# Dummy matmuls up to and between the first transposes, and two small matmuls moved into the last output matmuls of block 0

## The chip, the cores and the metric

The kernel runs on one core of a Trainium2 chip. The metric is the device time of one execution in microseconds (us), as the median of several runs. The engines are TensorE (PE; its weight loads are listed apart as PEld), VectorE (DVE), ScalarE (ACT), GpSimd (POOL) and SyncE (SP), which here only issues DMAs.

## What is computed

A linear attention is followed by a gated feed-forward layer, for 8 batches of 576 tokens with 8 heads of 64 (so 512 columns) and 1536 hidden units. Inputs and output are float32; the matmuls run in float16.

```python
q_s = exp(q) / sum(exp(q), axis=-1)            # over the 64 of a head
k_s = exp(k) / sum(exp(k), axis=2)             # over the 576 tokens
kv  = einsum('bhsd,bhse->bhde', k_s, v)
x   = einsum('bhsd,bhde->bhse', q_s, kv)       # rows: 8*576 tokens of 512
out = (gelu(x @ w_gate) * (x @ w_val)) @ w_out
```

## The kernel before, in words

Every batch has 512 main tokens and 64 remaining ones. A "block" is the feed-forward of one batch's main tokens; block 8 holds the remaining tokens of all batches. The order is 0 to 6, 8, 7.

**Attention of a batch b.** `exp` (L139) runs on ACT and writes eq (from q) and ek (from k). `norm` (L170) divides eq by its row sums, a head pair hp at a time: `norm_sum` (reduce and reciprocal, always DVE) and `norm_mul` (L165, DVE or POOL). `cast_v` (L148) makes v float16 on DVE, ACT or POOL; on POOL, spans of more than two heads are cut into calls of two. `unit_kv(b, g)` (L189) has 10 matmuls, 5 for each of two head pairs, into the PSUM tile pskv, then on DVE one reciprocal rck and two kv_sb. `unit_t(b, g)` (L213) transposes the eq of two head pairs with 8 transposes on PE into pst, and copies pst to eqt. `unit_x(b, hp)` (L242) is one matmul of kv_sb with eqt into psx, then a cast to xt on the engine named. g=0 are the lower heads (hp 0 and 1), g=1 the upper ones.

**Feed-forward of a block.** For each of 12 slices fi of the hidden units there are 4 matmuls into psg and 4 into psv (L266 to L269), then `gate` (L271): Gelu on ACT, and a product on DVE that gives ht. `ffn_first` (L286) begins blocks 0 and 1: it runs the halves of several slices that need only xt of hp 0 and 1, and calls the rest of the batch's attention in between. Then come the output matmuls (L310): for each of 4 row groups ns, 12 matmuls into psy, and `evac` (L345), which scales psy into yo; two row groups are stored together. Block 0 does all four row groups in two passes: fi 0 to 5 for each, then fi 6 to 11 for each (L491 to L500).

**Order of the work.** It is written out by hand: each engine runs its instructions in the order in which the program issues them. Pieces of other batches' work are put behind named points: `at(b, FI, i, ...)` behind slice i of block b, `at(b, NS, i, ...)` behind row group i, and `ride` (L476) calls them. In block 0, `NS` points 4 to 7 come behind the four row groups of the second pass. All loads go through SP in one order, with 5 buffers for q, k and v and 8 for staged weights. The weight casts are on POOL.

**The start (L386 to L415).** `warm_pe(n)` (L257) issues n matmuls of 512 columns with the identity as weights and zeros as data; nothing reads their result. Before, 16 of them come first, then the 8 transposes of the lower heads of batch 0, 6 more dummies, the 8 transposes of the upper heads, 20 matmuls of `unit_kv`, 4 of `unit_x`, and block 0.

PSUM has 6 banks for the tiles named "mm" (psg, psv, psy, pswarm, and psx where `big` is set) and 2 for the attention's.

Of the kernel before, what the change touches and what calls it, by code (L numbers as in the profile page):

```python
# [11 lines left out]
ACTF = mybir.ActivationFunctionType  # L12
ALU = mybir.AluOpType

_H_SCALE = 1024.0
# [3 lines left out]
def kernel(  # L19
# [10 lines left out]
    nc = tc.nc  # L30
# [6 lines left out]
    NFI = F // P  # L37
# [79 lines left out]
    def copy_on(eng, dst, src):  # L117
        if eng == "pool":
            nc.gpsimd.tensor_copy(out=dst, in_=src)  # L119
        elif eng == "act":  # L120
            nc.scalar.copy(out=dst, in_=src)  # L121
        else:
            nc.vector.tensor_copy(out=dst, in_=src)  # L123
# [15 lines left out]
    def exp(nm, b, h0=0, h1=H, n0=0, parts=((1, NC), (0, 1))):  # L139

        dst = (ek_b if nm == "k" else eq_b)[b % 2]
        for c0, c1 in parts if nm == "k" else ((n0, NC),):
            nc.scalar.activation(  # L143
                out=dst[:, c0:c1, h0 * D:h1 * D].rearrange("p n (h d) -> p h n d", d=D),
                in_=tiles[(nm, b)][:, h0:h1, c0 * D:c1 * D].rearrange("p h (n d) -> p h n d", d=D),
                func=ACTF.Exp, bias=kbias[:, 0:1] if c1 == 1 else 0.0)

    def cast_v(b, h0, h1, eng="pool"):  # L148
        if eng == "pool" and h1 - h0 > 2:
            for h in range(h0, h1, 2):  # L150
                cast_v(b, h, h + 2)
            return
        copy_on(eng, v16_b[b % 2][:, :, h0:h1, 0:D].rearrange("p n h d -> p h n d"),
                tiles[("v", b)][:, h0:h1, :].rearrange("p h (n d) -> p h n d", d=D))
# [15 lines left out]
    def norm(b, hp, eng="dve", n0=0):  # L170
        norm_sum(b, hp, n0)
        norm_mul(b, hp, eng)
# [16 lines left out]
    def unit_kv(b, g):  # L189
        pskv = ps_att.tile([P, 2, 2 * VW], f32, name="pskv", tag="att")  # L190
        for j in range(2):
            hp = 2 * g + j
            for n in range(NC):
                nc.tensor.matmul(  # L194
                    pskv[:, j, :], ek_b[b % 2][:, n, hp * P:(hp + 1) * P],
                    v16_b[b % 2][:, n, 2 * hp:2 * hp + 2, 0:VW],
                    start=(n == 0), stop=(n == NC - 1))
        rck = att.tile([P, 2], f32, name="rck", tag="rck")
        nc.vector.reciprocal(out=rck, in_=pskv[:, :, D])
        for j in range(2):  # L200
            kv_sb = att.tile([P, 2, D], f16, name="kv_sb", tag="kv", bufs=12)
            nc.vector.scalar_tensor_tensor(  # L202
                out=kv_sb,
                in0=pskv[:, j, :].rearrange("p (h e) -> p h e", e=VW)[:, :, 0:D],
                scalar=rck[:, j:j + 1], in1=mask, op0=ALU.mult, op1=ALU.mult)
            st[(b, "kv", 2 * g + j)] = kv_sb
# [6 lines left out]
    def unit_t(b, g, eng="dve"):  # L213
        eqt = get_eqt(b)
        pst = ps_att.tile([P, 2, MAIN], f16, name="pst", tag="att")
        for j in range(2):
            hp = 2 * g + j
            for n in range(NM):
                nc.tensor.transpose(  # L219
                    pst[:, j, n * P:(n + 1) * P],  # L220
                    eq_b[b % 2][:, n + 1, hp * P:(hp + 1) * P], ident)
        copy_on(eng, eqt[:, 2 * g:2 * g + 2, 0:MAIN], pst)
# [14 lines left out]
    def get_xt(b):  # L237
        if (b, "xt") not in st:
            st[(b, "xt")] = att.tile([P, HP, MAIN], f16, name="xt", tag="xt")
        return st[(b, "xt")]  # L240
# [16 lines left out]
    def warm_pe(n):  # L257
        ps = ps_big.tile([P, 512], f32, name="pswarm", tag="mm")
        for _ in range(n):
            nc.tensor.matmul(ps, ident, warm, start=True, stop=True)  # L260
# [18 lines left out]
    def ffn_fi(xt, fi):  # L279
        psg = ps_big.tile([P, 512], f32, name="psg", tag="mm")  # L280
        mm_gv(psg, wg_sb, xt, fi, range(HP))
        psv = ps_big.tile([P, 512], f32, name="psv", tag="mm")
        mm_gv(psv, wv_sb, xt, fi, range(HP))
        return gate(psg, psv)
# [25 lines left out]
    def mm_out(psy, hts, ns, fis):  # L310
        for fi in fis:
            nc.tensor.matmul(psy, hts[fi][:, ns * P:(ns + 1) * P], wo_sb[:, fi, :],  # L312
                             start=(fi == 0), stop=(fi == NFI - 1))
# [4 lines left out]
    def store(eng, src, b, n0, n1, c0=0, c1=C):  # L318
        base = out_rows(b)[:, 1 + n0:1 + n1, c0:c1]
        (pm, nm), (pn, _), _ = base.ap  # L320
        last = [[1, (n1 - n0) * C]] if c1 - c0 == C else [[1, c1 - c0]]
        eng.dma_start(out=bass.AP(tensor=base.tensor, offset=base.offset,
                                  ap=[[pm, nm], [NM * pn, 2]] + last), in_=src)
# [18 lines left out]
                    nc.scalar.activation(out=yl, in_=ps[i], func=ACTF.Copy, scale=1.0 / _H_SCALE)  # L342
                store(nc.scalar if i == 2 else nc.sync, yl, b, ns, ns + 1, c0, c1)

    def evac(b, ns, psy):  # L345
        if ns % 2 == 0:
            yo_t[b] = yop.tile([P, 2, C], f32, name="yo", tag="yo")
        yo = yo_t[b][:, ns % 2, :]
        if b == B:
            nc.vector.tensor_scalar(out=yo, in0=psy, scalar1=1.0 / _H_SCALE,  # L350
                                    scalar2=None, op0=ALU.mult)
            for j in range(2):
                nc.sync.dma_start(
                    out=out[(2 * ns + j) * S:(2 * ns + j + 1) * S, :].rearrange(
                        "(m n) c -> m n c", n=NT)[:, 0, :],
                    in_=yo[j * 64:(j + 1) * 64, :])
            return
        nc.vector.tensor_scalar(out=yo, in0=psy, scalar1=1.0 / _H_SCALE,  # L358
                                scalar2=None, op0=ALU.mult)
        if b == order[-1]:  # L360
            store(nc.sync, yo, b, ns, ns + 1)
        elif ns % 2 == 1:
            store(nc.sync, yo_t[b].rearrange("p n c -> p (n c)"), b, ns - 1, ns + 1)
# [24 lines left out]
    exp("q", 0, 4, 8, 1)  # L388
    exp("k", 0, 0, 4)
    exp("k", 0, 4, 8)  # L390
    warm_pe(16)
    norm(0, 0, "dve", 1)
    norm(0, 1, "pool", 1)
    norm(0, 2, "dve", 1)
    norm(0, 3, "pool", 1)
    unit_t(0, 0, "dve")
    warm_pe(6)
    cast_v(0, 0, 4, "dve")
    cast_v(0, 4, 6, "act")
    unit_t(0, 1, "act")  # L400
    cast_v(0, 6, 8, "dve")
    unit_kv(0, 0)
    unit_kv(0, 1)
    cast_w("wg", 0, "pool")
# [13 lines left out]
    FI, NS = 0, 1  # L418
    plan = {}

    def at(b, kind, i, *fns):
        plan.setdefault((b, kind, i), []).extend(fns)

    L = lambda f, *a: (lambda: f(*a))
# [3 lines left out]
       L(norm, 1, 0), L(norm, 1, 1, "pool"), L(norm_sum, 1, 2), L(norm_mul, 1, 2, "pool"),  # L428
       L(cast_v, 1, 0, 4, "act"), L(exp, "k", 1, 4, 8))
    at(0, NS, 5, L(unit_t, 1, 0))  # L430
    at(0, NS, 6, L(unit_kv, 1, 0), L(cast_v, 1, 4, 6, "act"), L(cast_v, 1, 6, 8),
       L(norm, 1, 3, "pool"))
    at(0, NS, 7, L(unit_x, 1, 0, "act", True), L(unit_x, 1, 1, "act", True),
       L(preload, ACTF.Gelu))
    first1 = [[L(unit_kv, 1, 1), L(unit_t, 1, 1)], [L(unit_x, 1, 2, "act")],
              [L(unit_x, 1, 3, "dve")]]
    first = {0: [[], []], 1: first1}
# [38 lines left out]
    def ride(b, kind, i):  # L476
        for fn in plan.get((b, kind, i), []):
            fn()

    for b in order:  # L480
        xt = get_xt(b) if b < B else xtr
        hts = []
        fi0 = 0
        if b in first:
            hts = ffn_first(xt, first[b])
            fi0 = len(hts)
            ride(b, FI, fi0 - 1)
        for fi in range(fi0, NFI):
            hts.append(ffn_fi(xt, fi))
            ride(b, FI, fi)  # L490
        if b == 0:  # L491
            psys = []
            for ns in range(4):
                psys.append(ps_big.tile([P, C], f32, name="psy", tag="mm"))
                mm_out(psys[ns], hts, ns, range(0, NFI // 2))
                ride(b, NS, ns)
            for ns in range(4):
                mm_out(psys[ns], hts, ns, range(NFI // 2, NFI))
                evac(b, ns, psys[ns])
                ride(b, NS, 4 + ns)  # L500
        else:
            for ns in range(4):
                if b == order[-1] and ns == 3:
                    last_rows(b, hts, ns)
                    break
                psy = ps_big.tile([P, C], f32, name="psy", tag="mm")
                mm_out(psy, hts, ns, range(NFI))
                evac(b, ns, psy)
                ride(b, NS, ns)
# [30 lines left out]
```

The softmax here doesn't subtract the row's maximum and nothing guards it: scores larger than these inputs give would overflow.

## Times and profile before

| what | value |
|---|---|
| median of 5 runs | 329.17 us (328.57 to 330.06) |
| the profiled execution | 329.04 us, span 327.2 us |
| PE busy | 317.6 us (97%) |
| DVE, ACT, POOL busy | 180.1, 147.3, 45.2 us |
| mean DMA rate over the span | 154 GB/s |

The span runs from the first to the last instruction. A matmul's record ends later than the next one begins, since they are pipelined, so spacing is read from the chain or from starts. In the timeline, a row gives the start, the length, the engine, the line, the operation, what is written and read, the number of merged instructions, and in brackets the idle time of the engine before it with what ended it. The granted TensorE clock is a share of full speed.

### The profile page before, as it was taken

The page shows a single profiled execution, that of the slowest core. Times are in us where ns is not written, and L with a number is a line of the kernel's source. Part 1 is how long each engine was busy: PE and PEld are TensorE (multiplying, and loading weights), DVE is VectorE, ACT ScalarE, POOL GpSimd, SP SyncE. Part 2 cuts the span into 40 slices and gives each one's busy share as a digit, 9 for nine tenths or more (in the row PEclk, how much of TensorE's full clock was granted, in tenths as well). Part 3 has the DMA queues.
Part 4 walks back from the last instruction along what each step waited for, and adds up shares of the span by engine and source line. Part 5 has one row for each costly group of instructions (what it writes and reads, how often), then busy time and mean ns, then how long its engine had stood idle before and what let it go on. Part 6 is the DMA issues. An engine that isn't in the chain of part 4 may idle for free.

```text
span 327.2 us, 4529 instructions
## 1 busy us (share of the span) xinstructions
PE 317.6 (97%) x1726; PEld 154.4 (47%) x1726; DVE 180.1 (55%) x327; ACT 147.3 (45%) x197; POOL 45.2 (14%) x58
## 2 busy tenths in 40 slices
PE   7699999999999999999999999999999999999995
PEld 2444444445454544544454445444544444444444
DVE  2743465497579736962597339732983234324431
ACT  3553584898344572349134932484243033103310
POOL 1477451303001200030004000300000000000000
PEclk9599999999999999999999999999999999999999
DMA  7999999960186015900591039301100110041002
GB/s 226 365 385 392 401 393 390 394 250 0 64 301 247 2 65 188 358 2 8 172 387 45 2 128 366 118 0 66 64 0 2 64 64 2 0 99 29 3 33 96
DMA packets 38502, 50.49 MB, mean 154 GB/s; under 512 B 2128, under 2 KB 34256, under 8 KB 38480
## 3 DMA queue, kind: packets, MB, share of 16 engines
q1 hardware_dynamic: 38336, 50.14, 43.1%
q8 instruction: 13, 0.21, 0.3%
q10 hardware_dynamic: 144, 0.07, 0.1%
q14 instruction: 9, 0.07, 0.1%
HBM read 40.76 MB, written 9.44 MB: 153 GB/s over the span
## 4 chain that ended last, share of the span: by engine, by line
PE 89%; DMA 3%; ACT 3%; issue 2%; DVE 2%; POOL 0%; SPq 0%; ACTq 0%; POOLq 0%
PE psy L312 28%; PE psg L268 26%; PE psv L268 26%; PE pskv L194 3%; PE pst L219 2%; PE psx L246 2%; DMA out_dram<-yo 2%; DMA qt<-in_q_dram 2%; PE psl L333 1%; ACT L143 1%; PE pswarm L260 1%; ACT L273 1%; ACT eq L143 1%; DVE kv_sb L202 0%; PE pstr L231 0%
## 5 line engine op out<-in xcount | busy, mean ns | idle before, releaser
L273 ACT ACTIVATE gl<-psg 128x512 f32<-128x512 f32 x108 | 63.9, 598 | 137.4 <-PE psg L268 130.6
L275 DVE SCALAR_TENSOR_TENSOR ht<-psv,gl 128x512 f16<-128x512 f32 x108 | 73.9, 688 | 65.8 <-PE psv L268 63.7
L268 PE MATMUL psg<-xt,wg_sb 128*128 128x512 f16 x384 | 100.6, 379 | 0.7 <-ACT xt L121 0.5
L268 PE MATMUL psv<-xt,wv_sb 128*128 128x512 f16 x384 | 100.2, 379 | 0.1
L312 PE MATMUL psy<-wo_sb,ht 128*128 128x512 f16 x420 | 93.2, 379 | 0.0
L268 PEld LDWEIGHTS <-wv_sb 128*128 128x128 f16 x432 | 42.2, 98 | 51.9 <-issue 1.3
L312 PEld LDWEIGHTS <-ht 128*128 128x128 f16 x420 | 40.5, 98 | 46.9
L268 PEld LDWEIGHTS <-wg_sb 128*128 128x128 f16 x432 | 40.9, 98 | 44.9 <-issue 1.6
L358 DVE TENSOR_SCALAR yo<-psy 128x512 f32<-128x512 f32 x31 | 21.2, 687 | 49.1 <-PE psy L312 49.1
L119 POOL CAST v<-vt 128x640 f16<-128x640 f32 x25 | 18.9, 796 | 140.8 <-DMA vt<-in_v_dram 133.1
L160 DVE TENSOR_REDUCE rq<-eq 128x10 f32<-128x640 f16 (+1 forms) x32 | 25.3, 790 | 10.3 <-ACT eq L143 10.3
L167 DVE TENSOR_TENSOR eq<-eq,rrq 128x640 f16<-128x640 f16 (+1 forms) x27 | 23.4, 865 | 0.9
L121 ACT CAST xt<-psx 128x512 f16<-128x512 f32 x27 | 15.1, 587 | 17.7 <-PE psx L246 17.7
L143 ACT ACTIVATE eq<-qt 128x2560 f16<-128x2560 f32 (+1 forms) x9 | 18.3, 2049 | 4.4 <-DMA qt<-in_q_dram 4.4
L143 ACT ACTIVATE ek<-kt 128x2048 f16<-128x2048 f32 (+1 forms) x10 | 15.6, 1559 | 3.4 <-DMA kt<-in_k_dram 3.3
L219 PE MATMUL pst<-ident,eq 128*128 128x128 f16 x128 | 10.7, 228 | 3.6 <-DVE eq L167 2.1
L219 PEld LDWEIGHTS <-eq 128*128 128x128 f16 x128 | 8.9, 102 | 8.0 <-ACT eq L143 2.6
L194 PEld LDWEIGHTS <-ek 128*128 128x128 f16 x160 | 10.9, 101 | 3.3 <-issue 0.2
L194 PE MATMUL pskv<-v,ek 128*128 128x130 f16 x160 | 12.4, 226 | 0.0
L268 PE MATMUL psg<-xtr,wg_sb 128*128 128x512 f16 x48 | 12.3, 379 | 0.0
L268 PE MATMUL psv<-xtr,wv_sb 128*128 128x512 f16 x48 | 12.3, 379 | 0.0
L246 PE MATMUL psx<-eqt,kv_sb 128*128 128x512 f16 x32 | 10.8, 380 | 0.3 <-DVE eqt L123 0.2
(55 smaller groups left out, 138.2 us busy)
## 6 DMA issues: line engine op xcount, KB each, us to landing
kt<-in_k_dram SPq DMA_DIRECT2D x14, 640.0 KB, 7.9
vt<-in_v_dram SPq DMA_DIRECT2D x14, 640.0 KB, 9.2
qt<-in_q_dram SPq DMA_DIRECT2D x14, 640.0 KB, 6.6
out_dram<-yo SPq DMA_DIRECT2D x14, 512.0 KB, 3.0
wost<-in_moe_w_out_dram SPq DMA_DIRECT2D x6, 512.0 KB, 8.6
wgst<-in_moe_w_gate_dram SPq DMA_DIRECT2D x5, 512.0 KB, 7.4
wvst<-in_moe_w_val_dram SPq DMA_DIRECT2D x5, 512.0 KB, 7.8
kt<-in_k_dram SPq DMA_DIRECT2D x4, 320.0 KB, 8.7
```

The lines of the kernel that those rows point to most:

```text
L119: nc.gpsimd.tensor_copy(out=dst, in_=src)
L143: nc.scalar.activation(out=dst[:, c0:c1, h0 * D:h1 * D].rearrange("p n (h d) -> p h n d", d=D), in_=tiles[(nm, b)][:, h0:h1, c0 * D:c1 * D ...
L160: nc.vector.reduce_sum(rq, e, axis=mybir.AxisListType.X)
L167: (nc.gpsimd if eng == "pool" else nc.vector).tensor_tensor(out=e, in0=e, in1=rrq.unsqueeze(-1).to_broadcast((P, n, 2, D)), op=ALU.mult)
L194: nc.tensor.matmul(pskv[:, j, :], ek_b[b % 2][:, n, hp * P:(hp + 1) * P], v16_b[b % 2][:, n, 2 * hp:2 * hp + 2, 0:VW], start=(n == 0), sto ...
L219: nc.tensor.transpose(pst[:, j, n * P:(n + 1) * P], eq_b[b % 2][:, n + 1, hp * P:(hp + 1) * P], ident)
L246: nc.tensor.matmul(psx, st[(b, "kv", hp)].rearrange("p h e -> p (h e)"), st[(b, "eqt")][:, hp, 0:MAIN], start=True, stop=True)
L268: nc.tensor.matmul(ps, w[:, ci, fi * P:(fi + 1) * P], xt[:, ci, :], start=(ci == 0), stop=(ci == HP - 1))
L273: nc.scalar.activation(out=gl, in_=psg, func=ACTF.Gelu)
L275: nc.vector.scalar_tensor_tensor(out=ht, in0=psv, scalar=_H_SCALE, in1=gl, op0=ALU.mult, op1=ALU.mult)
L312: nc.tensor.matmul(psy, hts[fi][:, ns * P:(ns + 1) * P], wo_sb[:, fi, :], start=(fi == 0), stop=(fi == NFI - 1))
L358: nc.vector.tensor_scalar(out=yo, in0=psy, scalar1=1.0 / _H_SCALE, scalar2=None, op0=ALU.mult)
```

## The change

At the start the first run of dummies has 35 matmuls, not 16; the second has 9, not 6; and a third run of 2 is added between the upper heads' transposes (with the last cast of v) and `unit_kv`.

At the end of block 0, `unit_kv(1, 0)` now comes ahead of `evac` of row group 2, not behind it. The cast of v of heads 4 to 7 of batch 1 is wholly on POOL (heads 4 and 5 were on ACT, 6 and 7 on POOL). The product of `norm(1, 3)` is on DVE, not POOL. `unit_x(1, 0)` and `unit_x(1, 1)` stand between the matmuls fi 8 and fi 9 of row group 3, not behind its evacuation. That evacuation is on ACT, not DVE. The table of Gelu is still loaded last.

```diff
-    def evac(b, ns, psy):
+    def evac(b, ns, psy, eng="dve"):
...
-        nc.vector.tensor_scalar(out=yo, in0=psy, scalar1=1.0 / _H_SCALE,
-                                scalar2=None, op0=ALU.mult)
+        if eng == "act":
+            nc.scalar.activation(out=yo, in_=psy, func=ACTF.Copy, scale=1.0 / _H_SCALE)
+        else:
+            nc.vector.tensor_scalar(out=yo, in0=psy, scalar1=1.0 / _H_SCALE,
+                                    scalar2=None, op0=ALU.mult)
...
-    warm_pe(16)
+    warm_pe(35)
...
-    warm_pe(6)
+    warm_pe(9)
...
     cast_v(0, 6, 8, "dve")
+    warm_pe(2)
     unit_kv(0, 0)
...
-    at(0, NS, 6, L(unit_kv, 1, 0), L(cast_v, 1, 4, 6, "act"), L(cast_v, 1, 6, 8),
-       L(norm, 1, 3, "pool"))
-    at(0, NS, 7, L(unit_x, 1, 0, "act", True), L(unit_x, 1, 1, "act", True),
-       L(preload, ACTF.Gelu))
+    at(0, NS, 16, L(unit_kv, 1, 0), L(cast_v, 1, 4, 8))
+    at(0, NS, 6, L(norm, 1, 3))
+    at(0, NS, 17, L(unit_x, 1, 0, "act", True), L(unit_x, 1, 1, "act", True))
+    at(0, NS, 7, L(preload, ACTF.Gelu))
...
             for ns in range(4):
-                mm_out(psys[ns], hts, ns, range(NFI // 2, NFI))
-                evac(b, ns, psys[ns])
+                cut = 9 if ns == 3 else NFI
+                mm_out(psys[ns], hts, ns, range(NFI // 2, cut))
+                ride(b, NS, 14 + ns)
+                mm_out(psys[ns], hts, ns, range(cut, NFI))
+                evac(b, ns, psys[ns], "act" if ns == 3 else "dve")
                 ride(b, NS, 4 + ns)
```

## The prediction, as it was put on record

> **What bounds the kernel now.** I read the page first: busy shares, then the 40 slices (each 8.2 us).
>
> ```profile
> PE 317.6 (97%) x1726; PEld 154.4 (47%) x1726; DVE 180.1 (55%) x327; ACT 147.3 (45%) x197; POOL 45.2 (14%) x58
> ...
> PEclk9599999999999999999999999999999999999999
> DMA  7999999960186015900591039301100110041002
> ```
>
> PE is the bound, and its clock falls to half in the second slice alone. DMA is full in slices 2 to 8, to about 66 us, so early work may hang on transfers. The list of waits has only 0.5 us and 0.2 us of PE idle after 40 us, both near 50 us; from 76 us on the chain is PE nearly throughout. What is saved before 76 us is therefore saved at the end.
>
> Next, PE's timeline at the start, and the stages by the granted clock (last columns: clock, DMA share, GB/s).
>
> ```profile
> 1.36 6.02 PE L260 MATMUL pswarm<-warm,ident 128*128 128x512 f16 x16 [1.36 <-POOL ident masks.py:199]
> 9.48 0.45 PE L219 MATMUL pst<-ident,eq 128*128 128x128 f16 x4 [2.10 <-DVE eq L167]
> 11.42 0.61 PE L219 MATMUL pst<-ident,eq 128*128 128x128 f16 x4 [1.49 <-POOL eq L167]
> 11.82 2.77 PE L260 MATMUL pswarm<-warm,ident 128*128 128x512 f16 x6
> 14.38 1.06 PE L219 MATMUL pst<-ident,eq 128*128 128x128 f16 x8
> ```
>
> ```profile
> 9.60:9.80 0.20, 0.20 (x4) 0.09 (x2) 0.20 (x1) 0.00 (x0) 0.00 (x0) 0.64 1.05 390
> 9.80:10.00 0.20, 0.14 (x2) 0.00 (x0) 0.17 (x2) 0.00 (x0) 0.00 (x0) 0.50 1.06 390
> ...
> 16.40:16.60 0.20, 0.18 (x4) 0.06 (x1) 0.04 (x1) 0.09 (x1) 0.18 (x1) 0.79 1.04 364
> ```
>
> After the 16 dummies PE idles 2.10 us and then 1.49 us. A mean of 0.64 puts the fall at 9.66; 0.79 puts the rise at 16.48. The clock column says 1.00 before 4 us, yet the first dummies start 0.43 us apart (their weight loads at 5.60 and 6.03), the later ones 0.22: I go by spacing, and the first rise is near 6.3.
>
> Prices, from the chain and these rows: a 512-column matmul takes 0.216 us at full clock (36 in 7.77) and 0.427 at half (6 in 2.56); 8 transposes 0.52 and 0.85; 10 kv matmuls 0.57 and 1.10.
>
> **Part 1, the start.** Of the 35 dummies, 12 start at half clock as now and the 13th at 6.39; the 35th then starts at 6.39 + 22 x 0.216 = 11.14, and the slot ends at 11.36. Head pair 0's transposes have waited since 9.4, pair 1's wait for POOL until 11.42 anyway: four by 11.62, four by 11.88 (now 12.03). Nine dummies: 1.94, to 13.82 (now 14.59). Four transposes to 14.08; those of pair 3 wait for POOL's product,
>
> ```profile
> 12.89 1.04 POOL L167 TENSOR_TENSOR eq<-eq,rrq 128x512 f16<-128x512 f16 x1 [1.53 <-DVE rrq L162]
> 14.10 1.23 DVE L123 CAST v<-vt 128x1280 f16<-128x1280 f32 x2 [0.80 <-DMA vt<-in_v_dram]
> ```
>
> ready at 13.98, so four more to 14.34 (now 15.44). The two new dummies: 0.43, to 14.77. The first kv matmuls then wait for v: it lands at 14.1, the first of the two casts takes 0.83 (by tile), so 14.97. **This, not PE, is late next**; 0.20 of the dummies' cost is cover. Ten matmuls at full clock end at 15.54; now the chain has 15.44 + 1.10 = 16.54. **Gain 1.00 us.** What follows (rck, kv_sb, psx, xt) hangs on DVE's kv_sb in the same spacing and shifts whole: psg from 18.41 to 17.41. The copy of eqt on ACT ends near 15.84 (after its cast at 14.81, 1.01 long), needed at about 16.9. The weights come from POOL's casts, which wait for DMA and don't move: the tightest is wv's third piece, 19.87 + 1.04 = 20.91, needed at 22.83 - 1.00 = 21.83, so 0.9 is left. PSUM: a third dummy tile only turns the banks by one; no row shows PE waiting for a bank here, so I take nothing.
>
> The size rests on when the clock rises and falls. If it rises at t (6.3 here), the 35 end at 0.494t + 8.24, and kv starts at the later of 14.97 and 0.494t + 11.65. Up to 6.7 nothing is lost, at 8.75 the gain is gone. The rows show two rises: 4.9 us after the first dummy, and 16.48, 5.1 us after the pair-1 transposes at 11.42, from which PE was busy. So I take 6.3. For the fall: PE has no idle over 0.4 us in my schedule until psg, so I take none; were kv at half clock, 0.53 would go.
>
> The Trainium skill ("TensorE: Matmul & The Clock Gate", Why this matters for your kernels) says that only idle gaps over about 3 us bring the half clock back. By it the 2.10 us gap would be harmless, the stretch to 16.48 would be at full clock already, and this part would gain only what the half-clock rows cost in other ways, near nothing. The row with 0.50 decides against it here. The same page (Part 1) says the window of about 3.4 us runs freely; by its figures the rise lies between 3.4 and 6.8 us after the first dummy, an estimate of 4.8 to 8.2, and the gain between 1.0 and 0.3 from run to run.
>
> **Part 2, the end of block 0**, first in the times of before.
>
> ```profile
> 48.82 0.74 PE L194 MATMUL pskv<-v,ek 128*128 128x130 f16 x10
> 49.39 1.46 PE L312 MATMUL psy<-wo_sb,ht 128*128 128x512 f16 x6
> 50.69 0.59 PE L246 MATMUL psx<-eqt,kv_sb 128*128 128x512 f16 x2
> 51.74 0.86 PE L268 MATMUL psg<-xt,wg_sb 128*128 128x512 f16 x2 [0.46 <-ACT xt L121]
> ```
>
> The two psx end PE's queue, and block 1 waits for their casts (1.07 for both on ACT, from 51.11): its first matmul starts at 51.74, its second, by the chain, at 52.23. After: kv ends at 49.56, three psy to 50.21. DVE's rck and kv_sb (49.63 to 50.43, about 0.3 each) come first in its queue as evac is now behind them; psx 0 starts at 50.2, psx 1 at 50.5 (a new wait of 0.1 on PE; behind it three psy and all of block 1), three psy to 51.37. A psx is ready 0.42 after its start: casts 50.62 to 51.69, second psg matmul at 51.74, **0.49 earlier**. Of the casts' 1.07 all but 0.15 lies under psy.
>
> DVE then does evac 2 (0.69, to 51.12), sum and reciprocal of norm 3 (1.07), and its product (0.83 by the 128x640 rows; POOL's took 1.26): done 53.05. PE's psv ends at 52.39, kv(1,1) at 52.96, and its last four transposes start at 53.22, so no wait. rck starts at 53.07 instead of 53.65, kv_sb ends at 53.87, eqt's copy (0.68) at 54.55, psx 2 at 54.60 instead of 55.12: **0.52** reaches block 1. The casts of v on POOL: 48.59, twice 0.72, so 50.05, needed at 52.39. evac 3 on ACT is in no row of this shape: bounds 0.28 (ACT's 128x128) and 0.69 (DVE's), nearest ACT's 0.59 for casting 128x512; with the table load of 1.28 behind it ACT is done by 53.8, and its next cast, of psx 2, is due at 55.0. Were Copy to need a table load of its own, 1.28 more would reach 55.1: 0 to 0.1. I take 0. SP's stores keep their order and go out at 53.70, after both evacuations.
>
> With Part 1's shift, do the inputs follow? q of batch 1: ACT's exp would start at 39.48; a weight issued later in the same queue had landed by 39.27. The lower v is cast by 46.46, kv(1,0) would start at 48.0; the upper by 50.05, kv(1,1) would start at 51.39 (52.39 less 1.00). So 0.2, 1.5 and 1.3 are left.
>
> **Sum.** 329.04 (profiled execution; span 327.2 and 1.84 around it) - 1.00 - 0.52 = **327.5 us**. The median is 0.13 above that execution; I don't add it, as it is inside the runs' spread.
>
> **Rivals.**
>
> (a) *The dummies run over.* The clock rises later than 6.7, and part of the 1.00 goes. From 6.7 to 8.75: 327.5 to 328.5, say 328.1. Against it: two rises at 4.9 and 5.1 us. For it: they are two in one execution. 0.16.
>
> (b) *Slower: dummies at half clock hold the transposes.* The same queue, beyond break-even: each us of delay costs 0.494, and with Part 2's 0.52 the whole is lost from a rise at 9.8 on. A rise at 12 lets kv start at 17.58 and end at 18.15 against 16.54: +1.61 - 0.52, so 330.1. If all 35 ran at half clock, kv would start at 16.30 + 0.85 + 3.84 + 0.85 + 0.85 = 22.7, some 6.6 us slower (335.7). Chance 0.05.
>
> (c) *A transfer hides it.* The chain names a DMA at 60.90:
>
> ```profile
> 55.27 5.63 DMA out_dram<-yo
> 60.90 1.28 ACT L143
> ```
>
> If exp of batch 2 truly waited there, neither gain would pass it: 329.0. Against: ACT's Gelu runs from 60.29 for 0.60, to 60.89, so ACT wasn't idle; and by tile these stores land 7.5 to 7.8 us after issue at 53.70 and 55.3, past 61. I read the row as a wrong name. 0.08.
>
> (d) *Part 2 gives nothing* (psx waits for kv_sb, or ACT's new evacuation gets before the casts): 329.04 - 1.00 = 328.0. 0.11.
>
> The forecast keeps 0.60.
>
> **Range and chances.** Low: 327.5 less the runs' own 0.6 below their median, 326.9. High: the start's gain wholly lost, 329.04 - 0.52 = 328.5, with 0.1 of median above it, 328.6. Outside: (b), (c) and tails. A difference of 0.3% (0.99 us, so below 328.18) is about what a measurement of this kernel can tell from no change. Faster: 0.59 of the forecast, 0.06 of (a), 0.06 of (d): 0.71. Slower: 0.05, from (b). Same: 0.24.
>
> **What would show it.** PE's clock 1.00 from about 6.3 to the end; dummies ending near 11.4; kv's first matmul at about 15.0 waiting for DVE's cast, not PE; psg at 17.4. Near 49.2: three psy, two psx, three psy, and psg's second matmul at 50.7; psx 2 at 53.6. Wrong: spacing of 0.43 past the 12th dummy, a half clock after 9 us, ACT idle before exp of batch 2, or a PE wait for wv's pieces at 20 to 22.

## The result, and the profile after

The changed kernel takes 328.17 us (median of 23 runs, 327.64 to 329.57) against 329.02 us (45 runs, 328.40 to 330.06): ratio 0.9973 [0.9965, 0.9980], so 0.85 us faster, where 1.5 us was forecast. The profiled execution took 328.17 us, its span 326.4 (before: 329.04 and 327.2).

From the page of the kernel after, the first line of busy shares and the slices of clock and DMA:

```profile
PE 320.0 (98%) x1750; PEld 155.2 (48%) x1750; DVE 180.2 (55%) x327; ACT 147.0 (45%) x197; POOL 44.8 (14%) x58
...
PEclk9999999999999999999999999999999999999999
DMA  7999999970196016900590039201100110041002
```

The 24 added matmuls are there (1750 against 1726), and the second slice's 5 has become a 9: the half clock after the first dummies is gone. PE is busier by 2.4 us and the span shorter by 0.8: the added busy time lies where PE used to wait.

PE's timeline at the start, after:

```profile
1.37 9.43 PE L260 MATMUL pswarm<-warm,ident 128*128 128x512 f16 x35 [1.37 <-POOL ident masks.py:199]
10.64 0.39 PE L219 MATMUL pst<-ident,eq 128*128 128x128 f16 x4
11.31 0.40 PE L219 MATMUL pst<-ident,eq 128*128 128x128 f16 x4 [0.29 <-POOL eq L167]
11.54 2.10 PE L260 MATMUL pswarm<-warm,ident 128*128 128x512 f16 x9
13.49 0.79 PE L219 MATMUL pst<-ident,eq 128*128 128x128 f16 x8
14.11 0.59 PE L260 MATMUL pswarm<-warm,ident 128*128 128x512 f16 x2
15.37 1.43 PE L194 MATMUL pskv<-v,ek 128*128 128x130 f16 x20 [0.66 <-DVE v L123]
...
17.96 0.72 PE L268 MATMUL psg<-xt,wg_sb 128*128 128x512 f16 x2
```

The two gaps of 2.10 and 1.49 us in front of the transposes have become one of 0.29. The last dummies end at 14.70; then PE waits 0.66 us for v. Block 0's first matmul starts at 17.96, not at 18.41: 0.45 earlier.

The chain of waits before, up to rck (start, length, what):

```profile
12.03 2.56 PE pswarm L260 x6
14.59 0.85 PE pst L219 x8
15.44 1.10 PE pskv L194 x10
16.54 0.02 issue
16.56 0.18 DVE rck L199
```

And after, from v on:

```profile
4.24 10.05 DMA vt<-in_v_dram
...
14.39 0.84 DVE v L123
15.23 0.14 issue
15.37 0.75 PE pskv L194 x10
...
16.14 0.18 DVE rck L199
```

Before, the chain was PE throughout from 12.03 to rck (dummies, transposes, kv). Now the transfer of v, 10.05 us long, leads to kv. rck starts at 16.14, not 16.56: 0.42 earlier.

PE's timeline at the end of block 0, after:

```profile
48.44 0.74 PE L194 MATMUL pskv<-v,ek 128*128 128x130 f16 x10
49.02 0.81 PE L312 MATMUL psy<-wo_sb,ht 128*128 128x512 f16 x3
49.83 0.65 PE L246 MATMUL psx<-eqt,kv_sb 128*128 128x512 f16 x2
50.32 0.81 PE L312 MATMUL psy<-wo_sb,ht 128*128 128x512 f16 x3
50.97 0.80 PE L268 MATMUL psg<-xt,wg_sb 128*128 128x512 f16 x2
...
54.27 0.38 PE L246 MATMUL psx<-eqt,kv_sb 128*128 128x512 f16 x1 [0.19 <-DVE eqt L123]
```

The two psx now stand between two threes of psy, and the wait of 0.46 for xt before block 1 is gone.

**Where the 0.87 of the two traces went.** Three starts of PE and the end say it: psg (the first of block 0), the six psy behind the transposes of batch 1 ("psy 2"), and psx 2 (the third psx of batch 1). From psx 2 to the end every traced execution takes the 273.9 us of before, within 0.2.

| kernel, trace | first psg | psg to psy 2 | psy 2 to psx 2 | psx 2 |
|---|---|---|---|---|
| before | 18.41 | 29.11 | 7.60 | 55.12 |
| after | 17.96 | 29.19 | 7.12 | 54.27 |
| gain | 0.45 | -0.08 | 0.48 | 0.85 |

### The profile page after: what moved, and what is told of

It reads as the page before. It is cut to its first block, busy times and chain, and to the rows that moved or that the text cites. A ratio compares the mean times of both kernels' runs of the same rounds, so it can differ in the third digit from the quotient of the medians.

```text
span 326.4 us, 4574 instructions
## 1 busy us (share of the span) xinstructions
PE 320.0 (98%) x1750; PEld 155.2 (48%) x1750; DVE 180.2 (55%) x327; ACT 147.0 (45%) x197; POOL 44.8 (14%) x58
## 4 chain that ended last, share of the span: by engine, by line
PE 90%; DMA 3%; ACT 2%; issue 2%; DVE 1%; SPq 1%; ACTq 0%; DVEq 0%
PE psy L312 28%; PE psg L268 27%; PE psv L268 27%; DMA vt<-in_v_dram 3%; PE pskv L194 3%; PE psx L246 2%; PE pst L219 2%; SPq L103 1%; PE psl L333 1%; ACT L143 1%; ACT L273 1%; PE pstr L231 1%; DVE kv_sb L202 0%; ACT gl L273 0%; DVE v L123 0%
## 5 line engine op out<-in xcount | busy, mean ns | idle before, releaser
L119 POOL CAST v<-vt 128x640 f16<-128x640 f32 x26 | 19.9, 804 | 142.9 <-DMA vt<-in_v_dram 105.5
L260 PE MATMUL pswarm<-warm,ident 128*128 128x512 f16 x46 | 12.1, 424 | 1.4 <-POOL ident masks.py:199 1.4
```

## The experiments

The theory after the result: both parts do what they say, and most of what the start falls short by is the arrival of v. The rivals: v hides the start wholly and block 0 brings all of the 0.85; or the dummies as such bring less than 1.00, v in time or not. Twelve kernels ran in three groups; each ratio is against the kernel before, run on the same chip. Medians of before in the groups: 329.13 (e1 to e4), 329.11 (e5 to e8), 328.84 (e9 to e12). This table, from the traces, goes with all of them ("v cast" is the start of DVE's first cast of v, "kv" that of the first kv matmul; e5, e6, e9 and e10 leave out the true v of batch 0, and the cast reads the tile of k instead, which is there):

| trace | us | v cast | kv | first psg | psg to psy 2 | psy 2 to psx 2 |
|---|---|---|---|---|---|---|
| e1 | 330.09 | 15.69 | 16.67 | 19.26 | 29.14 | 7.59 |
| e2 | 328.24 | 14.07 | 15.05 | 17.64 | 29.55 | 7.12 |
| e3 | 329.87 | 15.80 | 16.77 | 19.36 | 29.48 | 7.12 |
| e4 | 328.12 | 14.22 | 15.14 | 17.85 | 29.23 | 7.12 |
| e5 | 328.37 | 13.14 | 14.99 | 17.69 | 29.66 | 7.12 |
| e6 | 328.76 | 13.10 | 14.64 | 18.69 | 29.03 | 7.12 |
| e7 | 328.81 | 13.73 | 15.28 | 18.88 | 29.03 | 7.12 |
| e8 | 328.20 | 13.10 | 14.64 | 18.25 | 29.03 | 7.12 |
| e9 | 327.70 | 13.05 | 14.59 | 17.18 | 29.51 | 7.12 |
| e10 | 327.97 | 13.06 | 14.89 | 17.50 | 29.45 | 7.12 |
| e11 | 327.22 | 13.38 | 14.52 | 17.11 | 29.07 | 7.12 |
| e12 | 328.29 | 14.05 | 15.02 | 17.62 | 29.36 | 7.39 |

**e1: the dummies alone, on the kernel before.**

```diff
-    warm_pe(16)
+    warm_pe(35)
...
-    warm_pe(6)
+    warm_pe(9)
...
+    warm_pe(2)
     unit_kv(0, 0)
```

> Only the dummy matmuls are changed (35, 9 and 2); the end of block 0 is as before. Theory A (each part gives about half, and both reach the end): in the two traces the first transposes of batch 1 moved from 47.00 to 46.58, so 0.4 us less than before, about 328.6. Theory B (the transfers, which fill the DMA to 66 us, swallow the earlier start, and the end of block 0 alone made the whole difference): no difference from before, 329.0.

Measured: 329.10 us, 0.9991 [0.9971, 1.0012]; neither 0.4 us nor nothing is excluded. The trace says more. PE's timeline of e1:

```profile
13.84 0.59 PE L260 MATMUL pswarm<-warm,ident 128*128 128x512 f16 x2
16.67 1.43 PE L194 MATMUL pskv<-v,ek 128*128 128x130 f16 x20 [2.23 <-DVE v L123]
```

and DVE's:

```profile
15.69 1.66 DVE L123 CAST v<-vt 128x1280 f16<-128x1280 f32 x2 [2.77 <-DMA vt<-in_v_dram]
```

PE had done all its early work by 14.43, the clock was at 1.00, and all of it was lost in a wait of 2.23 us for a v whose cast could start only at 15.69. In this execution the dummies gave nothing: psg came at 19.26, 0.85 later than in the trace of before.

**e2: the end of block 0 alone, with the old dummies.** Its edit is the whole change but the dummies: `warm_pe(16)` and `warm_pe(6)` are kept, and the third run is left out.

> Only the end of block 0 is changed; the dummies are 16 and 6 as before. Theory A: psx 2 moved by 0.85 in the trace of the change, of which 0.42 was there before block 0 ended, so this part alone gives 0.43 us, about 328.6, and the gains of the two parts add up to the 0.85 of both. Theory B: this part alone gives the whole 0.85, about 328.2.

Measured: 328.39 us, 0.9972 [0.9951, 0.9992]. The interval takes in 0.4 as well as 0.85, so e1 and e2 together don't settle the shares by their times. By the medians alone e2 (0.9972) has the whole gain of the change (0.9973), and e1 (0.9991) nearly none: no time shows what the dummies are worth on average in the kernel as it is. The traces show the shares of one execution each: psy 2 to psx 2 is 7.12 with the edit (e2) and 7.59 without (e1), as in after and before. Part 2 is worth 0.48. And e2's psg starts at 17.64, earlier than that of the whole change, with the old dummies: its half clock ended at 13.8 (below) and its v came at 14.07.

**e3: the change with a first run of 16 dummies again.**

```diff
-    warm_pe(35)
+    warm_pe(16)
```

> The changed kernel with 16 dummies in the first run instead of 35; 9, 2 and block 0 stay as changed. Theory A (the long first run matters since it leaves no gap in which the clock falls): the clock falls near 9.7 as before; the pair-1 transposes end at 12.0, nine dummies at 0.427 take 3.84, eight transposes 0.85, two dummies and kv start near 17.2 instead of 15.37, so about 1.5 us slower than the change, 329.7, slower than before. Rival C (the gap of 2.1 us is harmless, the later dummies are enough): the same as the change, 328.2.

Measured: 329.61 us, 0.9994 [0.9976, 1.0011]. That is 1.21 above e4 of the same group and 1.44 above the change, but the intervals just overlap, and the trace again has a late v (15.80): by how much the 19 dummies are the part that counts stays open. e3's 12 runs fall into two groups by the mean granted clock of the execution (last section).

**e4: v cast by three engines.** After, DVE casts heads 0 to 3 and ACT heads 4 and 5; kv of heads 0 to 3 waits for DVE alone.

```diff
-    cast_v(0, 0, 4, "dve")
-    cast_v(0, 4, 6, "act")
+    cast_v(0, 0, 2, "dve")
+    cast_v(0, 2, 4, "act")
     unit_t(0, 1, "act")
-    cast_v(0, 6, 8, "dve")
+    cast_v(0, 4, 6, "dve")
+    cast_v(0, 6, 8, "pool")
```

> The changed kernel, with v of batch 0 cast in four pieces of two heads: heads 0-1 on DVE, 2-3 on ACT, 4-5 on DVE, 6-7 on POOL. Theory A (v's arrival at 14.4 and then DVE's cast of 0.93 set the start of kv): kv starts after a cast of 0.49, near 14.9 instead of 15.37, the second half's reciprocal no longer waits for DVE's second cast, and psx 0 comes near 16.2 instead of 16.75: 0.5 us less than the change, about 327.7. Rival D (casts on DVE and POOL at the same time stretch each other, or the weight casts behind v on POOL come late): no gain over the change, 328.2.

Measured: 328.40 us, 0.9962 [0.9943, 0.9981], not told apart from the change (0.9973). kv doesn't wait for v any more in its trace: it starts at 15.14, right behind the last dummies, because here the clock rose late (the dummies are 0.43 apart up to 7.3) and the transposes follow the 35 dummies at 11.88 instead of 10.64. So the wait for v goes and the dummies' own length is what comes last: the rival of dummies that run over. e5 and e7 below show the same, with transposes at 11.72 and 11.89.

**e5 and e6: v never late, with the new and the old dummies.** The casts of batch 0's v read the tile of k, which lands before v.

```diff
-                tiles[("v", b)][:, h0:h1, :].rearrange("p h (n d) -> p h n d", d=D))
+                tiles[("v" if b else "k", b)][:, h0:h1, :].rearrange("p h (n d) -> p h n d", d=D))
```

> The changed kernel, but the float16 v of batch 0 is cast from k's tile, which lands about 3 us earlier: the true v of batch 0 is left out (it is loaded and not used), so nothing waits for it. Now TensorE's own path (dummies, transposes) sets when kv starts. Theory E (in the changed kernel v's arrival sets the start of block 0, and the half clock cost the kernel before its full price only in some executions): psg starts near 17.2 to 17.8, less scattered than with v; about 0.4 to 0.6 us less than the change, 327.6. Theory A (as predicted, v at 14.1 and little scatter): also somewhat less, 327.8. The comparison with the next kernel decides.

> As the kernel before it, with the dummies of before (16, 6, none); the end of block 0 as changed. The true v of batch 0 is left out in the same way. Theory A (16 dummies let the clock fall, which costs about 1 us in every execution once v is out of the way): 1.0 us slower than with the new dummies. Theory E (the clock's fall and rise come at times that differ by up to 3.4 us between executions, and in the late ones the clock is back before kv): slower by 0.2 to 0.5 us only.

Measured: e5 327.93 us, 0.9965 [0.9953, 0.9977]; e6 328.83 us, 0.9997 [0.9987, 1.0007]. The 0.90 between them is not the dummies' worth. PE's timeline of e6:

```profile
14.64 1.18 PE L194 MATMUL pskv<-v,ek 128*128 128x130 f16 x10
16.82 0.73 PE L194 MATMUL pskv<-v,ek 128*128 128x130 f16 x10 [1.00 <-DVE kv_sb L202]
```

The second half of kv waits 1.00 us for DVE's kv_sb, in e5 it does not. These matmuls read nothing of kv_sb, so what they wait for can only be the PSUM tile that kv_sb reads: an inference, which the next group tests. The pair is confounded, and that group repeats it without this wait.

**e7 and e8: v loaded in two halves**, so that the first four heads land earlier; with the new and the old dummies.

```diff
-    for src, nm, n0 in ((q, "q", 1), (k, "k", 0), (v, "v", 0)):
+    for src, nm, n0 in ((q, "q", 1), (k, "k", 0)):
         load(src, nm, 0, 0, H, n0)
+    for h0 in (0, 4):
+        load(v, "v", 0, h0, h0 + 4, 0)
```

> The changed kernel with v of batch 0 loaded in two halves, heads 0 to 3 first, so that the first cast and the first kv matmuls need only half of v. Theory E: the lower half lands about 1.3 us earlier (0.59 MB at about 0.39 MB per us is 1.5 us), the first kv matmuls wait for TensorE and not for v in executions where v is early, and start some 1 us earlier where it is late: about 0.4 us less than the change, 327.8. Rival F (two more DMAs at the start push k or the weights back as much): no gain, 328.2.

> As the kernel before it, with the dummies of before (16, 6, none); the end of block 0 as changed. Theory E: with v in halves TensorE's path binds more often, so the dummies are worth 0.2 to 0.5 us here: slower than the kernel with the new dummies by that, about 328.1. Theory A: slower by 1.0 us.

Measured: e7 328.48 us, 0.9982 [0.9970, 0.9994]; e8 328.73 us, 0.9994 [0.9983, 1.0005]. Both show the same wait of 1.00. kv does start early (14.64 in e8), and what is won is given back in the wait. For v in halves this decides nothing; it wasn't tried without the wait.

**e9 and e10: e5 and e6 again, the second half of kv in a PSUM tile of the other pool**, so that the second half can't wait for the tile of the first. The wait of 1.00 is gone in both traces.

```diff
-    unit_kv(0, 1)
+    unit_kv(0, 1, True)
...
+        pskv = (ps_big if big else ps_att).tile([P, 2, 2 * VW], f32, name="pskv",
+                                                tag="mm" if big else "att")
```

> As the kernel with v taken from k's tile and the new dummies, with the second kv's PSUM tile in the pool of six banks, so that its matmuls wait neither for DVE's kv_sb of the first nor for ACT's copy of the transposes. The true v of batch 0 is left out. Theory E and A alike: near 327.8, a little below the kernel without the other bank; it is the reference for the next one.

> As the kernel before it, with the dummies of before (16, 6, none). The true v of batch 0 is left out. The earlier pair of this kind differed by 1.05 us, but the one with the old dummies had its second kv behind DVE's kv_sb of the first (1.00 us of TensorE idle in its trace), which is out of the way here. Theory E (the clock falls with the old dummies, but returns at a time that differs between executions): 0.2 to 0.5 us slower than with the new dummies. Theory A (1.0 us in every execution): 1.0 us slower. No difference would mean that the half clock costs nothing even when v is in time.

Measured: e9 327.84 us, 0.9970 [0.9959, 0.9981]; e10 328.33 us, 0.9985 [0.9974, 0.9997]. With v in time and no wait for a tile the dummies are worth 0.49 us in the medians and 0.32 at psg in the traces (17.50 against 17.18). The intervals of the two ratios overlap, but run against run e9 is the shorter in 97 of 108 pairs. The worth depends on how long the half clock of e10 lasts: its five runs with a mean clock of 0.993 to 0.995 have a median of 328.13, the seven with 0.990 one of 328.43, so 0.29 and 0.59 above e9 (last section). A gain of 1.0 us does not appear even then. In e9 nothing waits for v, and psg comes 0.78 before that of after; yet the time is only 0.47 below after's trace, since 0.32 more is lost between psg and psy 2. The last section shows where.

**e11: the change, the casts of e4, the second tile of e9, and the lower heads' second product of batch 1 on DVE**, and **e12: the change with this last edit alone**.

```diff
-       L(norm, 1, 0), L(norm, 1, 1, "pool"), L(norm_sum, 1, 2), L(norm_mul, 1, 2, "pool"),
+       L(norm, 1, 0), L(norm, 1, 1), L(norm_sum, 1, 2), L(norm_mul, 1, 2, "pool"),
```

> A version meant to beat the change: the changed kernel, with v of batch 0 cast in four pieces on DVE, ACT, DVE and POOL, the second kv in the pool of six banks, and the product of norm 1 of batch 1 on DVE instead of POOL. Theory G (after an earlier start the transposes of batch 1 wait for POOL's product of head pair 1, which gave back 0.1 to 0.6 us in four of the traces): it adds its 0.2 us to the 0.3 of the spread casts, about 327.6. Rival: the product on DVE delays the next sums and evacuations there and gives back what it gains: 327.9.

> The changed kernel with the product of norm 1 of batch 1 on DVE instead of POOL, nothing else. Theory G: head pair 1's eq is ready some 0.5 us earlier (DVE's product takes 0.83, POOL's 1.24), so the transposes near 46.6 do not wait: 0.1 to 0.3 us less than the change, about 328.0. Rival: v's arrival is the only thing that limits the earlier start: no difference from the change, 328.2.

Measured: e11 327.80 us, 0.9970 [0.9958, 0.9982]; e12 328.26 us, 0.9978 [0.9967, 0.9989]. Neither is told apart from the change. e11's trace is the shortest of all (327.22, psg at 17.11, only 29.07 to psy 2), but v landed early in it (13.38), so it isn't shown that its edits did this. e12 loses at another place. PE's timeline of e12:

```profile
49.93 0.65 PE L246 MATMUL psx<-eqt,kv_sb 128*128 128x512 f16 x2 [0.27 <-DVE kv_sb L202]
```

DVE has this product too (0.83 us from 45.87), and the one before it took 1.60 beside a cast on POOL (last section); so kv_sb starts at 49.53, not at 49.42, and the two psx inside row group 3 wait: psy 2 to psx 2 is 7.39 instead of 7.12. In e11, which has the product on DVE too but 1.02 for the one before it, they don't wait (7.12). This is the "new wait" that the prediction put at 0.1 in Part 2 and that the change itself doesn't show.

## Why the prediction was right or wrong

The time, 328.17, lies in the range; the forecast, 327.5, was 0.67 low. It is in the range since the upper end allowed for the whole of Part 1 to be lost, and more than half of it was. The gain of 0.85 is less than the 0.99 that the prediction took as the least that can be told from no change; with the runs there are, the interval of the ratio doesn't reach 1.

**Part 2 was right.** 0.52 was forecast, 0.48 (7.60 to 7.12) is in the trace of every kernel with the edit but e12. psy and psx interleave as said; the ACT evacuation took 0.62 where 0.59 was taken from the nearest row, and Copy loaded no table. The second psg matmul starts at 51.38 instead of 52.23.

**Part 1 was mis-sized: 1.00 was forecast, 0.45 came at psg and 0.37 past block 0.** The dummies did what was said or more: the transposes follow them at 10.64, where the forecast had 11.36, since the clock rose near 4.8 (by their spacing) and not at 6.3; the last dummies end at 14.70 against 14.77. The step that failed is "it lands at 14.1, the first of the two casts takes 0.83 (by tile), so 14.97. Ten matmuls at full clock end at 15.54". In the trace:

- v's cast started at 14.39, 0.29 later than before, and cast and issue took 0.98, where the forecast's 14.97 leaves 0.87 from 14.10: kv starts at 15.37, 0.40 late.
- The first ten matmuls end 0.75 after their start by the chain, not 0.57. The forecast put the spacing of ten in place of start to end, and so left out the 0.18 until the first result is there.

These make 0.58, and 1.00 less 0.58 is the 0.42 seen at rck. The prediction had named v as "late next", and had then taken its arrival as a fixed number from one execution. e1 shows what that is worth: with v at 15.69, nothing is left of the part. Nor is 1.00 to be had by an early v alone: with v in time the dummies give 0.49 (e9 and e10, both with the other PSUM tile).

**0.08 was given back in block 0**, which the prediction didn't see: it shifted everything from psg on as a whole. 0.05 of it are the eight transposes of batch 1 (0.57 in the chain, 0.52 before), the second four of which depend on POOL's product. In e2, e3, e5, e9 and e10 it is 0.34 to 0.55.

**The base was an execution of the dearer kind.** The half clock of the profile of before lasted 6.83 us; in the five other traces with a first run of 16 it lasted 3.42. What the dummies save depends on which of the two an execution gets, as the two groups of e10 show.

**The rivals.** (c), the transfer of the output that the chain named at 55.27, is out: everything before it moved by 0.85 and the exp of batch 2 moved by 0.84, to 60.06. The new chain doesn't name the DMA.

```profile
59.60 0.46 issue
60.06 1.28 ACT L143
```

(d) is out by 7.12 in place of 7.60. (b) has no sign in any trace. (a) is half true: part of the 1.00 went, as its time of 328.1 says, but in the trace of after by v and not by dummies that run over; the clock needed no rise later than 6.7 for the loss. Such a rise does come: in e4, e5 and e7, three of the eight traces with 35 dummies, where (a) had a chance of 0.16. In (b), the price for all 35 dummies at half clock was added up a little low: its own terms give 6.7 us and not 6.6.

## What to carry to other kernels

Dummy matmuls that keep the clock up are worth no more than the distance to the next thing that is late, here a transfer whose arrival varies by more than the whole gain: look at that arrival in several executions before pricing the part. A stall is removed for good only if nothing later is timed by the DMAs; work that arrives earlier at such a place may meet another engine's work and give part back. When a group of pipelined matmuls is put in a chain, take its length from its first start to its last result, as a chain row gives it where another engine released the group. A chain row behind other matmuls gives only the spacing: ten kv matmuls are 0.57 there, 0.75 from start to end.

## What the runs showed of the hardware

**The clock's half-speed stretch came in one length or its double.** The stage rows of e2, whole us each (us, busy of PE, PEld, DVE, ACT, POOL; clock, DMA share, GB/s):

```profile
10.00:11.00 1.00, 0.00 (x0) 0.00 (x0) 0.93 (x3) 0.28 (x1) 0.97 (x1) 0.70 1.04 370
11.00:12.00 1.00, 0.87 (x6) 0.59 (x7) 1.00 (x2) 1.00 (x2) 0.07 (x1) 0.50 1.06 389
12.00:13.00 1.00, 1.00 (x4) 0.40 (x3) 0.96 (x3) 1.00 (x2) 0.40 (x1) 0.50 1.07 395
13.00:14.00 1.00, 1.00 (x5) 0.33 (x3) 0.01 (x1) 0.52 (x2) 0.64 (x1) 0.59 1.11 355
```

A mean of 0.70 puts the fall at 10.40, 0.59 the rise at 13.82: 3.42 us. So do e3, e6, e8 and e10, each from another start (10.5 to 12.2); before has 6.83. The mean granted clock of a whole execution tells the two apart without a trace: 3.42 us at half speed in 327 give 0.995, twice that 0.990. Of the 95 executions of the kernel before beside the experiments, 40 have 0.992 to 0.995 and a median of 328.70 us; 50 have 0.988 to 0.990 and 329.16; 5 have 0.984, as three times 3.42 would give, and 330.90. e3's 12 runs split into 7 at 328.70 and 5 at 329.72. All executions with 35, 9 and 2 dummies have 0.998 or more but two: one of e1 (0.994, 331.14 us) and one of e7 that stands apart (0.658, 485.18 us). Thus Part 1 takes away a loss of clock that differs from run to run. The times still spread as widely, over 1.93 us in the 23 runs after and 1.66 in the 45 before.

PE's busy time goes with it. In the 3.42 us before the fall PE was busy for 0.18 to 0.38 of the time in the six traces with a first run of 16. In the kernel before it was busy for 0.56 of the next 3.41 us, and the half clock stayed; in the five others for 0.79 (e2) to 1.00 (e10), and it ended. Where between these the limits lie, no run shows.

The Trainium skill ("TensorE: Matmul & The Clock Gate", Part 1: The HAM clock gate) speaks of a free-running window of 3413 ns; the measured 3.42 and its double agree. The same page (Why this matters for your kernels) lets only idle gaps over about 3 us bring the half clock back; in the six traces with a first run of 16 no gap was longer than 2.71, yet the clock fell: in before behind a gap of 2.10 alone, in the others during or after a second one of 1.56. The measurement decides.

**The arrival of a first load varies by over 2 us.** With the same loads in the same order, the first cast of v, which waits for the transfer in all eight traces, started between 13.38 (e11) and 15.80 (e3). It goes with no edit: 14.39, 15.69, 14.22, 13.38 and 14.05 with 35 dummies, 14.10, 14.07 and 15.80 with 16. What decides it stays open.

**A product on DVE and a cast on POOL hold each other up, and the one that starts first wins.** In the kernel after, DVE's product and then POOL's last cast of output weights before it:

```profile
43.53 0.88 DVE L167 TENSOR_TENSOR eq<-eq,rrq 128x640 f16<-128x640 f16 x1
```

```profile
42.69 1.04 POOL L119 CAST wo_sb<-wost 128x1024 f16<-128x1024 f32 x1 [0.22 <-DMA wost<-in_moe_w_out_dram]
```

The same two in e12, where the product comes earlier against the cast:

```profile
43.19 1.60 DVE L167 TENSOR_TENSOR eq<-eq,rrq 128x640 f16<-128x640 f16 x1
```

```profile
43.07 1.04 POOL L119 CAST wo_sb<-wost 128x1024 f16<-128x1024 f32 x1 [0.23 <-DMA wost<-in_moe_w_out_dram]
```

The product ends 0.68 after the cast's end in both (44.41 and 43.73; 44.79 and 44.11), however early it starts; alone it takes 0.83. In e2, e3, e4, e5, e10 and e11 it is the same, within 0.01. In e9 the order is turned round, DVE first:

```profile
42.75 0.82 DVE L167 TENSOR_TENSOR eq<-eq,rrq 128x640 f16<-128x640 f16 x1
```

```profile
42.91 1.56 POOL L119 CAST wo_sb<-wost 128x1024 f16<-128x1024 f32 x1 [0.24 <-DMA wost<-in_moe_w_out_dram]
```

Now the product is as short as alone and the cast takes 1.56. The cast starts when its weights land, which doesn't move with PE. So a block 0 that is early against its weights runs its product into it (in e3, with the latest psg of all, the cast too is late, at 44.38), POOL's product for the transposes comes later, and in e2 the transposes wait:

```profile
46.96 0.40 PE L219 MATMUL pst<-ident,eq 128*128 128x128 f16 x4 [0.31 <-POOL eq L167]
```

That is 0.31 of the 0.44 by which e2's stretch from psg to psy 2 is longer than before's. PE's waits in this stretch account in the same way for 0.23 of e3's 0.37, 0.21 of e10's 0.34 and 0.53 of e5's 0.55. In e9, where the cast is the one held up, PE waits 0.29 for the cast weights instead, of 0.40. The rest of each is not traced. The Trainium skill ("SBUF — State Buffer", Who interferes with whom) has this as an exclusive lock: a DVE instruction with two inputs in SBUF and a GpSimd instruction that reads SBUF block each other, and the order of issue decides which waits. The three pairs above agree, with 0.83 grown to 1.60 and 1.04 to 1.56.

**A wait for a PSUM tile can come from an edit elsewhere.** In e6, e7 and e8 the second half of kv waited 1.00 us for DVE's kv_sb of the first, in no other kernel, though none of these edits touched that tile; in e10, with a tile of the other pool, the wait is gone. That the two halves shared a bank in the three is inferred; why the tiles fell so stays open.
